# First loads over two queues, an early weight load and late third query tiles at the start of an attention and gMLP kernel

## The chip, the cores and the metric

The kernel runs on one core of one Trainium2 chip. The metric is the device time of one execution in microseconds (us); lower is better. Profiles are of single executions, with times counted from the first instruction of the span. Below, PE is the engine of matmuls and transposes, DVE, ACT and POOL are the vector, scalar and GpSimd engines, SP is the engine that mostly issues transfers. POOL and ACT can issue transfers too; all transfers run on the same 16 DMA engines.

## What is computed

Grouped-query attention (8 batches, 16 query heads over 4 key and value heads, 384 positions, head dimension 64), then a gated MLP with a spatial gate over its output:

```python
scores = scale * np.matmul(q, k.transpose(0, 1, 3, 2))      # k, v repeated 4 times over heads
attn = softmax(scores)
x = np.matmul(attn, v) -> (batch, 384, 1024)
h = np.maximum(x @ w_in, 0.0)                                # w_in 1024 x 1024
u, v = h[..., :512], h[..., 512:]
v_n = (v - mean(v)) / np.sqrt(var(v) + 1e-06)
v_s = np.einsum('ts,bsd->btd', w_spatial, v_n) + b_spatial[None, :, None]
out = ((u * v_s) @ w_out)                                    # w_out 512 x 1024
```

Inputs and output are fp32; the matmuls work on fp16 copies.

## The kernel before

The scheduling is manual: each engine executes its instructions in the order in which the Python program emits them, and waits on semaphores where an operand, a buffer or an issued transfer isn't ready.

A batch has 6 sets: 3 query tiles `t` of 128 positions, times 2 pairs `j` of key heads. A set has 3 units, one for each key tile. A unit (`units`, L254) is two score matmuls (L268, one for each key head of the pair), followed by two exponentials on ACT (`exp`, L280). After the three units of a set, `weigh` (L282) multiplies the exponentials by the values (L288, two groups `hh` of 12 matmuls), and DVE takes a reciprocal (L301) and multiplies by it (L303): that gives a part of `x`. `x_turn` (L314) transposes `x` on PE and DVE copies it out of PSUM (L207). Then the MLP: `v_part` (L336, the second 512 columns of `w_in`, matmul L343), `u_part` (L397, the first 512 columns, L402), the spatial matmul (L421) and the output matmul (L453).

The MLP's matmuls are filler: the generator `gated` (L472) yields them one at a time and `pour` (L639) puts them between attention units so far as a budget in ns allows. The first 21 units run one at a time (loop at L660, `ALONE`). In that loop, work listed in `todo` for step `u` is emitted after the step's scores and exponentials. For the first batch, the first half of `v_part`'s contraction (4 of 8 steps) may be poured from step 7, the second half from step 10 (L478, L480).

The start, which the change touches:

- L136 to L143 load the first batch: a key load in two halves, the value load, and query loads by `part_q` (L117), one transfer for some heads `hs` and tiles `ts` of pair `j`. One query load is issued by ACT, all others by SP. The last two (L142, L143) hold tiles 1 and 2 of a pair, 512 KB each.
- `cast_k` (L173), `cast_q` (L187) and `cast_v` (L180) copy fp32 loads to fp16; the engine is an argument. L554 to L557 cast the first key half and the first query tile on DVE and the second key half on POOL.
- `k_turn` (L209) and `q_turn` (L223) transpose keys and queries on PE (L215, L229) and copy the result out of PSUM. `idle` (L546) emits matmuls whose result nobody reads.
- L564 to L587 are POOL's queue: it issues the load of `w_in` (`load_w_in`, L152; columns by half, rows by range of 128; fp32 to fp16 in the transfer) in four pieces, the loads of the second batch, and casts. `load_w_in(1, 0, 4)` holds what the first four `v_part` matmuls read, `load_w_in(1, 4, 8)` what the next four read.
- L588 to L611 list what each step of the first 21 gets in addition: casts on DVE, `q_turn` of each tile, `x_turn`.

Of the kernel before, what the change touches and what calls it, by code (L numbers as in the profile page):

```python
# [17 lines left out]
def kernel(  # L18
# [21 lines left out]
    NT = S // P  # L40
# [29 lines left out]
    pool, dve, act, sp = nc.gpsimd, nc.vector, nc.scalar, nc.sync  # L70
# [27 lines left out]
    stage = {}  # L98

    def stage_tile(n, b, j=None):  # L100
        shape = [P, 2, NT, G * D] if n == "q" else [P, HKV, NT * D]
        t = ld.tile(
            shape, FP32, name=f"{n}32_{b}_{j}", tag=f"{n}32", bufs=4 if n == "q" else 2
        )
        stage[n, b, j] = t
        return t

    def part(src, t, lo, hi, eng):
        eng.dma_start(t[:, lo:hi, :], src[lo:hi].rearrange("h (p t) d -> p h (t d)", t=NT))

    def load_k(b, eng=sp):
        part(k[b], stage_tile("k", b), 0, HKV, eng)

    def load_v(b, eng=sp):
        part(v[b], stage_tile("v", b), 0, HKV, eng)

    def part_q(b, j, hs, ts, eng):  # L117
        h0, h1, t0, t1 = hs[0], hs[-1] + 1, ts[0], ts[-1] + 1
        eng.dma_start(  # L119
            stage["q", b, j][:, h0:h1, t0:t1],  # L120
            q[b, 8 * j + 4 * h0 : 8 * j + 4 * h1].rearrange(
                "(h i) (c t r) d -> (i c) h t (r d)", i=G, t=NT, r=G
            )[:, :, t0:t1],
        )

    def load_q(b, j, eng=sp):
        stage_tile("q", b, j)
        part_q(b, j, (0, 1), (0, 1, 2), eng)
# [8 lines left out]
    part(k[0], k0, 0, 2, sp)  # L137
    part_q(0, 0, (0,), (0,), sp)
    part(k[0], k0, 2, 4, sp)
    part_q(0, 1, (0, 1), (0,), sp)  # L140
    part(v[0], v0, 0, HKV, sp)
    part_q(0, 0, (0, 1), (1, 2), sp)  # L142
    part_q(0, 1, (0, 1), (1, 2), sp)  # L143

    w_in16 = cst.tile([P, NK, DFF], FP16, name="w_in16")
    w_out16 = cst.tile([P, NM, DM], FP16, name="w_out16")
# [5 lines left out]
    def load_w_in(half, lo, hi):  # L152
        cols = slice(half * DH, (half + 1) * DH)
        pool.dma_start(
            w_in16[:, lo:hi, cols],
            moe_w_in[lo * P : hi * P, cols].rearrange("(t p) f -> p t f", p=P),
        )
# [12 lines left out]

    k16s, q16s, kTs, qTs = {}, {}, {}, {}

    def cast_k(b, eng, js=(0, 1)):  # L173
        if b not in k16s:
            k16s[b] = ld.tile([P, 2, NT, 2, D], FP16, name=f"k16_{b}", tag="k16")
        src = stage["k", b, None].rearrange("p (j h) (t d) -> p j t h d", h=2, t=NT)
        for j in js:
            eng.tensor_copy(k16s[b][:, j], src[:, j])

    def cast_v(b, eng, js=(0, 1)):  # L180
        g0, g1 = 2 * js[0], 2 * js[-1] + 2
        eng.tensor_copy(
            v1[b % 2][:, g0:g1, :, 0:D].rearrange("p g t d -> p (g t) d"),
            stage["v", b, None][:, g0:g1].rearrange("p g (t d) -> p (g t) d", t=NT),
        )

    def cast_q(b, j, eng, ts=None, hs=(0, 1)):  # L187
        if (b, j) not in q16s:
            q16s[b, j] = ld.tile([P, NT, G, 2, D], FP16, name=f"q16_{b}_{j}", tag="q16", bufs=4)
        t16 = q16s[b, j]  # L190
        src = stage["q", b, j].rearrange("p h t (r d) -> p h t r d", d=D)
        for hh in hs:
            if ts is None:
                eng.tensor_copy(t16[:, :, :, hh, :], src[:, hh])  # L194
            else:
                for t in ts:
                    eng.tensor_copy(t16[:, t, :, hh, :], src[:, hh, t])
# [313 lines left out]
    b32 = cst.tile([P, S], FP32, name="b32")  # L511
    ws32 = cst.tile([P, NT, S], FP32, name="ws32")
    ws16 = cst.tile([P, NT, NT, P], FP16, name="ws16")

    def load_spatial(eng):
        eng.dma_start(b32, moe_b_spatial.rearrange("(a s) -> a s", a=1).to_broadcast([P, S]))
        rows = moe_w_spatial.rearrange("(c t r) s -> r c t s", t=NT, r=G)
        for r in range(G):
            eng.dma_start(ws32[32 * r : 32 * r + 32], rows[r])

    def cast_spatial():
        pool.tensor_copy(
            bias_bc.rearrange("a (t r c) -> a t r c", t=NT, r=G),
            b32.rearrange("a (c t r) -> a t r c", t=NT, r=G),
        )
        for tt in range(NT):
            pool.tensor_copy(
                ws16[:, :, tt].rearrange("p s (r c) -> p s r c", r=G),
                ws32[:, tt].rearrange("p (c s r) -> p s r c", s=NT, r=G),
            )  # L530

    def send_spatial():
        sp.dma_start_transpose(
            wsT16.rearrange("p s (t c) -> p (s t) c", t=NT),
            ws16.rearrange("p s t c -> p (s t c)"),
        )
# [4 lines left out]
    def at(n, f, *args):  # L541
        todo.setdefault(n, []).append((f, args))

    idle_no = [0]

    def idle(count):  # L546
# [4 lines left out]
        for _ in range(count):  # L551
            nc.tensor.matmul(ps, ident16, ident16, start=True, stop=True)

    cast_k(0, dve, (0,))  # L554
    cast_q(0, 0, dve, (0,), (0,))
    cast_q(0, 0, dve, (0,), (1,))
    cast_k(0, pool, (1,))  # L557
    idle(28)
    k_turn(0, 0, act)
# [1 line left out]
    q_turn(0, 0, 0, dve)  # L561
    idle(8)

    load_w_in(1, 0, 4)  # L564
    cast_v(0, pool)
    load_w_in(1, 4, 8)
    cast_q(0, 1, pool, (1,))
    load_k(1, pool)
    load_q(1, 0, pool)
    cast_q(0, 1, pool, (2,))  # L570
    load_q(1, 1, pool)
    load_v(1, pool)
    load_w_in(0, 0, 4)
    load_w_in(0, 4, 8)
    pool.memset(b32[:, 0:1], 0.0)
    pool.memset(ws32[:, 0, 0:1], 0.0)
    load_spatial(sp)
    cast_k(1, pool)
    load_k(2, pool)
    cast_q(1, 0, pool)  # L580
    load_q(2, 0, pool)
    cast_q(1, 1, pool)
    load_q(2, 1, pool)
    cast_v(1, pool)
    load_v(2, pool)
    cast_spatial()
    send_spatial()  # L587
    at(2, cast_q, 0, 1, dve, (0,))  # L588
    at(2, k_turn, 0, 1, dve)
    at(2, idle, 16)  # L590
    for n, b, j, t in (
        (2, 0, 1, 0),
        (5, 0, 0, 1),
        (6, 0, 0, 2),
        (7, 0, 1, 1),
        (9, 0, 1, 2),
        (16, 1, 0, 0),
        (18, 1, 1, 0),
        (20, 1, 0, 1),
        (21, 1, 1, 1),  # L600
        (24, 1, 0, 2),
        (27, 1, 1, 2),
    ):
        at(n, q_turn, b, j, t, dve)
    at(2, idle, 8)
    at(3, cast_q, 0, 0, dve, (1,))
    at(4, cast_q, 0, 0, dve, (2,))
    at(15, k_turn, 1, 0, dve)
    at(18, k_turn, 1, 1, dve)
    for s in range(SETS):  # L610
# [128 lines left out]
```

## Time and profile before

| | us |
|---|---|
| median of 3 runs | 242.28 |
| lowest and highest | 241.59, 246.64 |
| the profiled execution | 242.07 |
| its span, first to last instruction | 240.2 |
| PE busy | 232.8 (97%) |
| ACT busy | 170.4 (71%) |
| DVE busy | 142.0 (59%) |
| POOL busy | 100.4 (42%) |

The granted clock of PE is 1.000 over the span. In the profile a line such as `6.34 0.50 POOL L178 CAST k<-k_None ...` gives the start, the duration, the engine, the line of the kernel, the operation and its operands; in brackets stands how long the engine was idle before it, and what released it. The chain of waits follows the work that ended last back to its start, each step to what released it. The time from issue to landing of a transfer is given in a list of its own.

### The profile page before, as it was taken

To read this page: it belongs to the slowest core of one execution; us is meant where nothing else is said; L and a number is where in the kernel's file an instruction comes from. 1 tells how busy PE (TensorE), PEld (TensorE's weight loads), DVE (VectorE), ACT (ScalarE), POOL (GpSimd) and SP (SyncE) were. 2 spreads that over 40 slices of the span, in tenths; PEclk is the share of its full clock that TensorE was granted. 3 is DMA by queue.
4 is the path that set the end of the run, shared out by engine and by line. 5 is a ranking of instruction groups with operands and counts; after the bars stand their busy time and mean duration, and the time that the engine had idled before them with its cause. 6 is when DMAs were issued, how large, how long until landed. Compare 5 with 4: busy or idle time off the path is not lost.

```text
span 240.2 us, 5910 instructions
## 1 busy us (share of the span) xinstructions
PE 232.8 (97%) x2322; PEld 124.9 (52%) x2322; DVE 142.0 (59%) x375; ACT 170.4 (71%) x348; POOL 100.4 (42%) x138
## 2 busy tenths in 40 slices
PE   7889999999999999999999999999999999999993
PEld 6554656554555455554455445555455445545541
DVE  1567767566536765475844767366744767467361
ACT  2889997888798678978797776987587776501211
POOL 1598758531554900367025810556013500370550
PEclk9999999999999999999999999999999999999999
DMA  5999999999999959996999499939922434240157
GB/s 145 312 269 320 262 360 135 178 232 274 318 146 317 275 154 183 290 244 167 174 256 264 140 220 263 312 115 155 237 42 44 112 120 122 44 175 4 59 202 263
DMA packets 65339, 47.47 MB, mean 198 GB/s; under 512 B 48160, under 2 KB 57440, under 8 KB 65312
## 3 DMA queue, kind: packets, MB, share of 16 engines
q1 hardware_dynamic: 61488, 39.10, 66.5%
q0 software_dynamic: 3680, 7.87, 13.5%
q8 instruction: 18, 0.29, 0.5%
q10 hardware_dynamic: 144, 0.13, 0.3%
q14 instruction: 9, 0.07, 0.1%
HBM read 25.95 MB, written 12.58 MB: 160 GB/s over the span
## 4 chain that ended last, share of the span: by engine, by line
PE 91%; DMA 5%; DVE 1%; SPq 0%; ACT 0%; issue 0%; POOL 0%
PE pu L402 18%; PE pv L343 18%; PE po L453 18%; PE sc L268 15%; PE av L288 14%; PE psp L421 7%; DMA w_in<-in_moe_w_in_dram 3%; DMA k_None<-in_k_dram 2%; PE qps L229 1%; DVE x L303 1%; PE xps L320 0%; DVE vr L357 0%; ACT osb L207 0%; DVE r L301 0%; SPq L119 0%
## 5 line engine op out<-in xcount | busy, mean ns | idle before, releaser
L280 ACT ACTIVATE aT<-sc 128x512 f16<-128x512 f32 x288 | 148.2, 610 | 32.9 <-PE sc L268 31.8
L288 PEld LDWEIGHTS <-aT 128*128 128x128 f16 x1152 | 47.7, 97 | 18.1 <-issue 2.3
L288 PE MATMUL av<-v,aT 128*128 128x65 f16 x1152 | 51.7, 193 | 0.7 <-DVE x L303 0.6
L343 PE MATMUL pv<-w_in,xt 128*128 128x512 f16 x192 | 50.8, 379 | 0.5 <-DMA w_in<-in_moe_w_in_dram 0.5
L453 PE MATMUL po<-w_out,gT 128*128 128x512 f16 x192 | 50.4, 379 | 0.0
L402 PE MATMUL pu<-xt,w_in 128*128 128x384 f16 x256 | 49.9, 326 | 0.0
L387 POOL TENSOR_SCALAR vn<-vr,rstd,nmr 128x512 f16<-128x512 f32 x23 | 17.7, 784 | 73.2 <-DVE nmr L382 39.6
L438 POOL TENSOR_TENSOR gT<-vs,uT 128x384 f16<-128x384 f32 x31 | 32.5, 1059 | 33.9 <-DVE r L301 17.1
L268 PE MATMUL sc<-qT,kT 64*128 64x512 f16 x288 | 42.3, 380 | 0.4 <-DVE qT L207 0.2
L303 DVE TENSOR_TENSOR x<-av,r 128x256 f16<-128x256 f32 x96 | 40.8, 425 | 3.3
L301 DVE RECIPROCAL r<-av 128x4 f32<-128x4 f32 x96 | 17.2, 179 | 43.0 <-PE av L288 42.8
L207 DVE COPY osb<-po 128x512 f32<-128x512 f32 x38 | 26.1, 686 | 17.2 <-PE po L453 17.2
L402 PEld LDWEIGHTS <-w_in 128*128 128x128 f16 x256 | 22.1, 97 | 17.1 <-issue 5.5
L413 ACT ACTIVATE uT<-pu 128x384 f16<-128x384 f32 x32 | 15.8, 494 | 16.3 <-PE pu L402 16.1
L453 PEld LDWEIGHTS <-gT 128*128 128x128 f16 x192 | 17.1, 97 | 17.5 <-issue 3.3
L343 PEld LDWEIGHTS <-xt 128*128 128x128 f16 x192 | 15.8, 97 | 18.4 <-issue 5.6
L194 POOL CAST q<-q 128x768 f16<-128x768 f32 x28 | 22.4, 832 | 6.5 <-DMA q<-in_q_dram 6.5
L268 PEld LDWEIGHTS <-kT 64*128 64x128 f16 x288 | 10.8, 94 | 25.1 <-issue 14.4
L421 PE MATMUL psp<-wsT,vn 128*128 128x384 f16 x96 | 22.2, 327 | 0.0
L433 DVE TENSOR_TENSOR vs<-psp,bias_bc 128x384 f32<-128x384 f32 x32 | 17.6, 552 | 7.1 <-PE psp L421 6.9
L357 DVE TENSOR_SCALAR vr<-pv 128x512 f32<-128x512 f32 x24 | 16.4, 683 | 8.4 <-PE pv L343 8.4
L369 DVE BATCH_NORM_STATS2 stats<-vr 128x6 f32<-128x512 f32 x24 | 16.4, 685 | 0.1
(44 smaller groups left out, 94.7 us busy)
## 6 DMA issues: line engine op xcount, KB each, us to landing
out_dram<-osb SPq DMA_DIRECT2D x21, 512.0 KB, 2.9
q<-in_q_dram SPq DMA_DIRECT2D x10, 768.0 KB, 7.4
q<-in_q_dram POOLq DMA_DIRECT2D x4, 768.0 KB, 10.5
v_None<-in_v_dram SPq DMA_DIRECT2D x6, 384.0 KB, 4.6
w_in<-in_moe_w_in_dram POOLq DMA_DIRECT2D x4, 512.0 KB, 11.0
k_None<-in_k_dram SPq DMA_DIRECT2D x5, 384.0 KB, 3.9
out_dram<-osb SPq DMA_DIRECT2D x6, 256.0 KB, 2.2
q<-in_q_dram SPq DMA_DIRECT2D x2, 512.0 KB, 7.7
```

The costliest lines, as they stand in the source:

```text
L194: eng.tensor_copy(t16[:, :, :, hh, :], src[:, hh])
L207: (act.copy if eng is act else dve.tensor_copy)(o, i)
L268: nc.tensor.matmul(sc, kTs[b][rows, j, kt * P : (kt + 1) * P], qTs[b, j][rows, qt].rearrange("p (r i c) -> p i r c", r=G, i=G), start=True ...
L280: act.activation(a, sc, AF.Exp, scale=scale)
L288: nc.tensor.matmul(av[:, i * (D + 1) : (i + 1) * (D + 1)], aT[:, kt, hh, i * P : (i + 1) * P], v1[b % 2][:, 2 * j + hh, kt, 0 : D + 1], st ...
L303: dve.tensor_tensor(x16s[b][:, qt, c : c + 256].rearrange("p (i d) -> p i d", i=G), o[:, :, 0:D], r.to_broadcast([P, G, D]), ALU.mult,)
L343: nc.tensor.matmul(pv, xts[b][:, kt, st * P : (st + 1) * P], w_in16[:, kt, DH:DFF], start=(kt == 0), stop=(kt == NK - 1),)
L387: (dve if b == 0 and st == 1 else pool).tensor_scalar(vn, v_r.pop((b, st)), rstd[:, st : st + 1], nmr[:, st : st + 1], op0=ALU.mult, op1=A ...
L402: nc.tensor.matmul(pu[:, 0:S], w_in16[:, kt, m * P : (m + 1) * P], xts[b][:, kt, :], start=(kt == 0), stop=(kt == NK - 1),)
L421: nc.tensor.matmul(psp[:, 0:S], v_n[b, st][:, m * P : (m + 1) * P], wsT16[:, st, :], start=(st == 0), stop=(st == NT - 1),)
L438: pool.tensor_tensor(gT, vs, uT, ALU.mult)
L453: nc.tensor.matmul(po, gTs[b][:, m, tt * P : (tt + 1) * P], w_out16[:, m, half * 512 : (half + 1) * 512], start=(m == 0), stop=(m == NM - 1),)
```

## The change

Five edits at the start of the program:

1. The first tile of query pair 1 is issued by ACT, behind ACT's first load, and no longer by SP.
2. SP's last two query loads hold tile 1 alone (256 KB each). Tile 2 of both pairs is loaded by `rest_q`, emitted at step 2: DVE writes one element of the target in each partition (a memset), and SP's transfer, which overwrites it, waits for that memset.
3. The cast of the first key half is split over its two heads: POOL casts the second head, DVE the first.
4. `load_w_in(1, 0, 4)` stands on POOL right behind its part of that cast, ahead of POOL's cast of the second key half.
5. In the list of steps the third tiles are later: `q_turn` of pair 0's tile 2 at step 10 (was 6) and of pair 1's at step 12 (was 9), pair 1's tile 1 at step 6 (was 7), and DVE's cast of pair 0's tile 2 at step 7 (was 4). The rest of POOL's queue from `cast_q(0, 1, pool, (2,))` on is emitted at step 3 and not before the loop; its order stays.

```diff
     part(k[0], k0, 2, 4, sp)
-    part_q(0, 1, (0, 1), (0,), sp)
+    part_q(0, 1, (0, 1), (0,), act)
     part(v[0], v0, 0, HKV, sp)
-    part_q(0, 0, (0, 1), (1, 2), sp)
-    part_q(0, 1, (0, 1), (1, 2), sp)
+    part_q(0, 0, (0, 1), (1,), sp)
+    part_q(0, 1, (0, 1), (1,), sp)
...
-    def cast_k(b, eng, js=(0, 1)):
+    def cast_k(b, eng, js=(0, 1), hs=slice(0, 2)):
...
-            eng.tensor_copy(k16s[b][:, j], src[:, j])
+            eng.tensor_copy(k16s[b][:, j, :, hs], src[:, j, :, hs])
...
+    def rest_q(j):
+
+        dve.memset(stage["q", 0, j][:, 0:1, NT - 1, 0:1], 0.0)
+        part_q(0, j, (0, 1), (NT - 1,), sp)
...
-    cast_k(0, dve, (0,))
+    cast_k(0, pool, (0,), slice(1, 2))
+    load_w_in(1, 0, 4)
+    cast_k(0, dve, (0,), slice(0, 1))
     cast_q(0, 0, dve, (0,), (0,))
     cast_q(0, 0, dve, (0,), (1,))
     cast_k(0, pool, (1,))
...
-    load_w_in(1, 0, 4)
     cast_v(0, pool)
     load_w_in(1, 4, 8)
     cast_q(0, 1, pool, (1,))
     load_k(1, pool)
     load_q(1, 0, pool)
-    cast_q(0, 1, pool, (2,))
-    load_q(1, 1, pool)
...
+    def behind_rest():
+        cast_q(0, 1, pool, (2,))
+        load_q(1, 1, pool)
...
+    at(3, behind_rest)
...
         (2, 0, 1, 0),
         (5, 0, 0, 1),
-        (6, 0, 0, 2),
-        (7, 0, 1, 1),
-        (9, 0, 1, 2),
+        (10, 0, 0, 2),
+        (6, 0, 1, 1),
+        (12, 0, 1, 2),
...
+    at(2, rest_q, 0)
+    at(2, rest_q, 1)
     at(3, cast_q, 0, 0, dve, (1,))
-    at(4, cast_q, 0, 0, dve, (2,))
+    at(7, cast_q, 0, 0, dve, (2,))
```

More of the change, by code (lines that the diff above doesn't have):

```diff
@@ L569 @@
     load_q(1, 0, pool)
-    cast_q(0, 1, pool, (2,))
-    load_q(1, 1, pool)
[L572 to L587, printed above, removed]
+    def behind_rest():
+        cast_q(0, 1, pool, (2,))
+        load_q(1, 1, pool)
+        load_v(1, pool)
+        load_w_in(0, 0, 4)
+        load_w_in(0, 4, 8)
+        pool.memset(b32[:, 0:1], 0.0)
+        pool.memset(ws32[:, 0, 0:1], 0.0)
+        load_spatial(sp)
+        cast_k(1, pool)
+        load_k(2, pool)
+        cast_q(1, 0, pool)
+        load_q(2, 0, pool)
+        cast_q(1, 1, pool)
+        load_q(2, 1, pool)
+        cast_v(1, pool)
+        load_v(2, pool)
+        cast_spatial()
+        send_spatial()
+    at(3, behind_rest)
     at(2, cast_q, 0, 1, dve, (0,))
```

## The prediction

> **What bounds the kernel now.** I read the page first, then busy time by stretch, then the chain of waits over the first 34 us, then the start on DVE and POOL and the single DMA issues there. All in us. The profiled execution took 242.07 with a span of 240.2; its sum is the base here. The median of the three runs shown is 242.28, 0.21 above it.
>
> Busy time by stretch (start:end, length, then busy time and count per engine, granted clock, DMA share, GB/s):
>
> ```profile
> 6.46:15.27 8.81, 7.29 (x99) 4.67 (x100) 5.42 (x18) 8.18 (x16) 6.15 (x11) 1.00 1.13 268
> 15.27:36.00 20.73, 20.67 (x265) 11.12 (x266) 14.14 (x44) 18.78 (x37) 14.98 (x24) 1.00 1.12 319
> 36.00:235.00 199.00, 198.75 (x1910) 104.56 (x1908) 120.34 (x309) 140.78 (x293) 78.33 (x97) 1.00 0.77 182
> ```
>
> From 15.27 to 235 PE idles 0.3 in all, at a granted clock of 1.00. So PE is the bound after 15.27, and the end moves by what PE starts earlier there, less what work is pushed behind that point. Ahead of it much of PE's busy time is filler (`idle`). The chain says what ended the start:
>
> ```profile
> 1.76 4.52 DMA k_None<-in_k_dram
> 6.28 0.05 issue
> 6.34 0.45 POOL k L178
> 6.78 8.35 DMA w_in<-in_moe_w_in_dram
> 15.13 0.14 issue
> 15.27 0.38 PE pv L343
> ```
>
> The first half of w_in's second 512 columns is issued by POOL behind the cast of the second key half, lands at 15.13 and releases the first `pv` matmul. PE's own wait there is only 0.5; the other paths arrive shortly before. These are on DVE and POOL:
>
> ```profile
> 10.53 0.90 DVE L197 CAST q<-q 128x256 f16<-128x256 f32 x4 [1.18 <-DMA q<-in_q_dram]
> 11.56 0.42 DVE L303 TENSOR_TENSOR x<-av,r 128x256 f16<-128x256 f32 x1
> 11.90 0.41 DVE L207 COPY qT<-qps 128x512 f16<-128x512 f16 x1
> ...
> 6.34 0.50 POOL L178 CAST k<-k_None 128x384 f16<-128x384 f32 x1 [4.91 <-DMA k_None<-in_k_dram]
> 6.78 0.96 POOL L154 DMA_DIRECT2D w_in<-in_moe_w_in_dram  x1
> ...
> 9.98 0.75 POOL L154 DMA_DIRECT2D w_in<-in_moe_w_in_dram  x1
> 11.92 0.75 POOL L197 CAST q<-q 128x256 f16<-128x256 f32 x2 [1.19 <-DMA q<-in_q_dram]
> ```
>
> DVE waited 1.18 and POOL 1.19 for the query loads, so those are nearly as late as w_in. The DMA issues (each asked for alone; last number: issue to landing) give the landings: q pair 0 at 3.26 + 7.2, pair 1 at 3.81 + 8.1 = 11.9, w_in's loads at 15.1 and 17.7, b at 17.84 + 8.0.
>
> ```profile
> q<-in_q_dram SPq DMA_DIRECT2D x1, 256.0 KB, 4.9
> q<-in_q_dram SPq DMA_DIRECT2D x1, 512.0 KB, 7.2
> q<-in_q_dram SPq DMA_DIRECT2D x1, 512.0 KB, 8.1
> w_in<-in_moe_w_in_dram POOLq DMA_DIRECT2D x1, 512.0 KB, 8.4
> w_in<-in_moe_w_in_dram POOLq DMA_DIRECT2D x1, 512.0 KB, 7.7
> b<-in_moe_b_spatial_dram SPq DMA_DIRECT2D x1, 192.0 KB, 8.0
> ```
>
> DMA share is 1.13 in 6.46 to 15.27: the DMA engines are full, so an earlier load pushes another back. What they moved, over 0 to 30 in 40 slices of 0.75:
>
> ```profile
> GB/s 0 0 22 234 359 243 82 220 341 350 374 395 369 258 212 197 190 169 180 200 326 354 347 380 363 377 389 391 307 292 214 229 262 279 252 257 231 216 255 332
> ```
>
> Query loads run at up to 395, w_in alone (from 10.5) at 170 to 210.
>
> **The change, part by part.**
>
> *Key cast split, w_in behind half of it.* The first key half lands at 4.03. DVE's cast of it (0.55) halves, POOL does the other half in about 0.25 (half of 0.50). w_in is issued at about 4.03 + 0.25 = 4.3 instead of 6.78. With its own latencies (7.7 to 8.35) it lands at 12.0 to 12.6; with all of the SP queue's remaining loads ahead, 14 at most, by my estimate. The first `pv` no longer waits for it unless everything else is over 1.3 earlier. POOL's second key cast now stands behind a 0.96 issue, which ends at 5.3, before its data at 6.28: free.
>
> *SP's order, ACT's second issue.* Third query tiles (512 KB of 1024 KB) leave the first queue; pair 1's first tile goes to ACT, behind an issue of 0.42, ahead of ACT's first copy at 5.17: ACT is free. SP's later issues come 0.5 earlier. The tile on ACT competes with the first key half and the first query tile. Bounds for the first exp (6.87 now): 0.1 earlier (shorter key cast, then the query casts) to 0.4 later (256 KB at the 359 GB/s peak of the DMA row, 0.7, half of it ahead). Neither is paid on: `av` of the first pair starts at 10.09 behind the value cast (ends 10.04), and the fifth exp it needs ends at 9.4, 0.6 before. 0.
>
> *Less on DVE before the first x.* Only the second tiles are cast at 10.53: two casts (0.49, as the pair at 4.50) for four (0.90). The reciprocal, `x` and `qT` copy behind them come 0.41 earlier if the query loads land as now.
>
> *The first pv.* PE ends the `av` ahead of it at 14.73 (14.20 + 0.53). Four transposes of a third tile (0.33 a group in the chain) move behind it: 14.40. DVE's 0.41: 13.99. The query loads are the unknown. Best, they are not slowed and each is half as large: 0.7 earlier (512 KB took 1.4, the distance of the two landings, and half of it goes). Worst, all 512 KB of w_in go ahead of the last of them: at the 190 GB/s of 11 to 14 in the DMA row that is 2.75, less the 1.4 of third tiles that no longer stand ahead, 1.4 later. I take 0.35 later, the middle: 14.34. So 15.27 - 14.34 = 0.93 earlier, of which 0.33 is work given back: **0.60 gained**.
>
> *The second w_in load.* It is issued as now, 9.98, because the value cast stands ahead of it. The same bytes as before have to pass ahead of it, so I leave it at 17.68. The fifth `pv` matmul, its first reader, starts at 18.62 now; with 0.60 gained and the other third-tile group (0.33) behind it, it is wanted at 17.69. It becomes the next limit, so the gain can't be much over 0.6: I charge 0.1. Bounds: 0 (0.7 sooner) and 0.6 (0.6 later, the whole gain).
>
> *Third tiles behind a memset on DVE.* Two memsets (0.06 each, as the one at 0.81) stand after the `qT` copy that ends at 9.35; SP issues at about 9.6 and 10.1 (0.5 each). In front of `r` and `x` of the second pair DVE now casts pair 0's third tile (0.49), in order. If it lands by 14.5, DVE is through in time. 256 KB took 4.9: 14.5. I charge 0.05; the upper bound is under the rivals. POOL's cast of the other third tile now waits too; behind it stand seven things (loads of batch 1's second queries and values, w_in's other half twice, two memsets, then SP's b and w_spatial). I estimate them 1 to 2 later. Readers with slack: w_in's other half landed by 32.4 for the first `pu` at 36, w_spatial's transpose landed at 40.1 for 44.7. 0, but only while POOL's queue still has a backlog of transfers, which it had until 32.
>
> **Sum:** 242.07 - 0.60 + 0.10 + 0.05 = **241.6**.
>
> **A rule against the change.** POOL's first w_in issue took 0.96 while DVE cast two query tiles beside it, one of which took 0.50 where the other casts took 0.29; the second issue, with DVE idle, took 0.75. In the new order the issue at 4.3 stands again beside DVE's two casts at 4.5, so 0.2 on each, within the cover of 0.6 above. The Trainium skill, "SBUF — State Buffer", section on SBUF's two separate sides, says that a DVE fp32 copy within SBUF can lock GpSimd out of a shared port for the whole instruction, so that descriptors can't be written. By that rule the issue could lose both casts, 0.57 instead of 0.2, and w_in would land by 13.2; the sum would not change, since the first `pv` is at 14.34.
>
> **Rivals.**
>
> *R1, slower: the third tile blocks DVE.* b, sent by SP while POOL's transfers filled the DMA engines, took 8.0 for 192 KB. If the third tile does too, it lands at 17.6; cast, reciprocal and `x` (0.49 + 0.18 + 0.42 and gaps, 1.15) end at 18.8. The scores that take over that bank start at 16.82 now and would be unmoved at 16.71 (one `pv` more, 0.22, one transpose group less, 0.33, ahead). With the second `x` behind, 2.3 lost: **244.4**. It decides from a latency of about 5.8 on (landing 15.4). For it: that row. Against: in b's case POOL had seven transfers in flight, here one or two.
>
> *R2, no change: w_in takes its room from the second query tiles.* Pair 1's land 1.4 later, at 13.3; POOL casts until 14.0, then transposes, turn of x, scores, `av` (0.33 + 0.33 + 0.32 + 0.48): first `pv` at 15.5, 0.2 later, plus 0.33 given back: **242.6**. For it: DMA share 1.13. Against: the two 512 KB query loads landed 1.4 apart, their full rate, although w_in had been issued 3.7 before the first of them landed. The Trainium skill, "DMA: Bandwidth & Descriptors", "Queues, rings and completion order", states that a DMA engine takes turns between the queues that have work; by that rule this rival is what would happen.
>
> *R3, more: both query loads come 0.7 earlier*, and the second w_in load 1.0, as the DMA engines lose less in the dip to 82 GB/s at 4.5: first `pv` at 13.3, so 1.97 less 0.33 gained, less the 0.1: **240.5**.
>
> *The change does nothing to w_in:* excluded, since nothing but the key half at 4.03 stands ahead of the issue.
>
> **From this to the numbers.** A measurement of this kernel tells about 2% (4.8) from no change. Forecast 241.6: chance 0.50. R2 242.6: 0.20. R1 244.4: 0.17, with its effect growing from 0 at a latency of 5.8. R3 240.5: 0.13. The range 240.4 to 243.4 holds the forecast, R2, R3 and R1 up to a latency of 7. Faster by over 2% would be under 237.4: 0.01. Slower by over 2%, over 247.1, would need a third tile 11 late: 0.03. Within: 0.96.
>
> **What would show it.** w_in's issue at 4.3 and landing at 12 to 14; first `pv` at 14.0 to 14.6, released by something other than w_in; two query casts on DVE at about 10.5; DVE's wait for the third tile under 0.5 and its landing by 14.5; PE without idle after 17.8. The prediction is wrong if DVE sits over 1 on that cast, if POOL's cast of pair 1 ends after 13.5, or if PE stalls later than 36, which nothing here foresees.

## The result, and the profile after

The changed kernel is slower: a median of 249.59 us (247.51 to 251.26, 6 runs) against 242.28 (241.59 to 246.64, 6 runs), a ratio of 1.0286 with a 95% interval of 1.0215 to 1.0357. I had forecast 241.6. The profiled execution took 251.26 (span 249.1), 9.2 over the 242.07 of the profiled execution of before; it is the highest of the six, so some 1.7 of that is this execution's own.

The ratios here leave out executions that are over 1.5% above the fastest of their kernel (the profiled one of the changed kernel is one, by a hair), which matters for E2, E3, E11 and E13, where the spread is given.

Busy time by stretch of the changed kernel; the columns are those of the same view of before, and the third stretch is new:

```profile
6.46:15.27 8.81, 8.46 (x115) 5.24 (x113) 4.93 (x16) 7.82 (x17) 4.26 (x7) 1.00 1.14 233
15.27:36.00 20.73, 17.61 (x241) 9.86 (x239) 14.14 (x44) 16.65 (x33) 13.33 (x22) 1.00 0.87 231
36.00:64.00 28.00, 23.30 (x229) 12.05 (x227) 14.07 (x40) 17.38 (x37) 14.07 (x19) 0.94 1.16 199
64.00:244.00 180.00, 179.75 (x1704) 93.90 (x1703) 107.72 (x274) 125.39 (x261) 66.79 (x82) 1.00 0.73 180
```

PE, which idled 0.06 from 15.27 to 36, now idles 3.1 there and another 4.7 between 36 and 64; behind 64 nothing is lost. DMA share in the second stretch fell from 1.12 to 0.87: the DMA engines themselves ran dry for a while. PE's own lines that carry a wait of 0.9 or more, with the first `pv` ahead of them:

```profile
14.13 0.59 PE L343 MATMUL pv<-w_in,xt 128*128 128x512 f16 x2
...
18.12 0.39 PE L268 MATMUL sc<-qT,kT 64*128 64x512 f16 x2 [2.16 <-DVE x L303]
...
27.11 0.40 PE L229 MATMUL qps<-ident,q 128*128 128x128 f16 x4 [0.96 <-POOL q L194]
```

```profile
55.00 0.38 PE L453 MATMUL po<-w_out,gT 128*128 128x512 f16 x1 [1.75 <-DMA w_out<-in_moe_w_out_dram]
...
58.27 1.46 PE L268 MATMUL sc<-qT,kT 64*128 64x512 f16 x6 [2.89 <-DMA qT<-q]
```

Four waits, 7.8 in all. The chain of waits names what stands behind them:

```profile
9.98 7.01 DMA q<-in_q_dram
17.02 0.50 DVE q L197 x2
17.64 0.44 DVE x L303
18.12 0.39 PE sc L268 x2
...
20.09 0.75 POOL q L197 x2
20.84 0.66 POOL q L119
...
26.21 0.86 POOL q L194
27.11 0.40 PE qps L229 x4
...
44.28 13.95 DMA qT<-q
58.27 1.46 PE sc L268 x6
```

The casts of the third tiles on DVE and POOL, and POOL's next load:

```profile
17.02 0.50 DVE L197 CAST q<-q 128x256 f16<-128x256 f32 x2 [3.06 <-DMA q<-in_q_dram]
...
20.09 0.75 POOL L197 CAST q<-q 128x256 f16<-128x256 f32 x2 [8.44 <-DVE qT L207]
20.78 0.72 POOL L119 DMA_DIRECT2D q<-in_q_dram  x1
```

The same load, and the transposes of batch 2's queries, in the kernel before:

```profile
14.74 0.72 POOL L119 DMA_DIRECT2D q<-in_q_dram  x1
...
39.98 9.79 SPq L246 DMA_TRANSPOSE qT<-q  x2
```

SP sends for pair 0's third tile at 9.98 and it lands 7.01 later; DVE, in order, sits on its cast for 3.06, and `x` and the scores come late. Pair 1's third tile lands at 19.97, after 9.5; POOL, in order, waits for it from 11.6 to 20.09. (The profile names a DVE copy that ended in the same moment; in E10 and E11 below the same cast starts 0.13 after its tile lands, too.) So POOL's next load (batch 1's second query pair) goes out at 20.78, where the kernel before issued it at 14.74: 6.0 later. All of POOL's queue is late from there, up to its casts for batch 2, which SP's transposes of batch 2's queries follow: the first is issued at 44.28, before at 39.98. It landed at 50.5 before, for scores that started at 50.67: 0.2 of slack. Now it lands at 58.2. Of these 7.8, 4.3 are the later issue; the other 3.5 are a longer transfer (13.95 for 10.49), and why is open.

The start of the n-th of the 288 exponentials on ACT, against the kernel before (a count in the two traces; positive is later), shows where the loss comes in:

| exponential | before | after | difference |
|---|---|---|---|
| 12 | 12.94 | 13.29 | +0.36 |
| 18 | 17.31 | 18.61 | +1.30 |
| 30 | 23.92 | 25.36 | +1.44 |
| 36 | 27.27 | 29.74 | +2.47 |
| 66 | 47.06 | 49.80 | +2.73 |
| 72 | 51.16 | 58.95 | +7.80 |
| 78 | 55.36 | 64.38 | +9.02 |
| 287 | 204.79 | 213.90 | +9.11 |

2.5 are lost by exponential 36 (start 27.27 before), on DVE's wait and on POOL's late casts for batch 1; 6.3 are lost between 49.8 and 64.4. The waits of PE there sum to 4.6. The rest is the clock:

```profile
58.00:60.00 2.00, 1.73 (x7) 0.43 (x7) 0.00 (x0) 1.05 (x3) 0.00 (x0) 0.50 1.25 271
60.00:62.00 2.00, 2.00 (x18) 1.14 (x17) 0.80 (x3) 2.00 (x5) 0.00 (x0) 0.67 0.93 271
```

The granted clock (the number behind the engines' busy times) is one half right after the idle time. By the clock records it is exactly 0.5 for 3.41 us, from 57.90 on, so 1.7 more. The Trainium skill, "TensorE: Matmul & The Clock Gate", section "What's actually happening", says that the clock halves after at least one idle window of about 3.4 us. The length agrees with these records, but here a window that was idle in part was enough. In each trace the clock changes on a grid of 3.41 us. In the window of that grid ahead of a fall to one half, PE idled 3.04 here, and 1.90 (E10), 2.42 (E12), 2.55 (E9), 2.73 (E5), 3.04 (E4) and 3.41 (E3) in the experiments below; after windows at full clock in which it idled 1.73 or less, the clock stayed. The wait of 2.16 ahead of 18.12 fell on two windows, 0.98 and 1.18, and halved nothing.

### The profile page after: what moved, and what is told of

It reads as the page before. It is cut to its first block, busy times and chain, and to the rows that moved or that the text cites. A ratio compares the mean times of both kernels' runs of the same rounds, so it can differ in the third digit from the quotient of the medians.

```text
span 249.1 us, 5917 instructions
## 1 busy us (share of the span) xinstructions
PE 235.2 (94%) x2322; PEld 125.7 (50%) x2322; DVE 142.6 (57%) x377; ACT 170.0 (68%) x348; POOL 100.5 (40%) x139
## 4 chain that ended last, share of the span: by engine, by line
PE 82%; DMA 10%; POOL 3%; DVE 2%; issue 1%; ACT 0%; SPq 0%; POOLq 0%
PE po L453 17%; PE pu L402 16%; PE pv L343 15%; PE sc L268 13%; PE av L288 12%; PE psp L421 6%; DMA qT<-q 6%; DMA q<-in_q_dram 4%; PE qps L229 1%; DVE x L303 1%; PE idle L557 1%; POOL w_in L154 0%; DVE qT L207 0%; POOL q L194 0%; DVE q L197 0%
## 5 line engine op out<-in xcount | busy, mean ns | idle before, releaser
L453 PE MATMUL po<-w_out,gT 128*128 128x512 f16 x192 | 51.1, 383 | 1.8 <-DMA w_out<-in_moe_w_out_dram 1.8
L268 PE MATMUL sc<-qT,kT 64*128 64x512 f16 x288 | 43.3, 385 | 5.4 <-DMA qT<-q 2.9
```

What stands on the lines that cost most here:

```text
L268: nc.tensor.matmul(sc, kTs[b][rows, j, kt * P : (kt + 1) * P], qTs[b, j][rows, qt].rearrange("p (r i c) -> p i r c", r=G, i=G), start=True ...
L453: nc.tensor.matmul(po, gTs[b][:, m, tt * P : (tt + 1) * P], w_out16[:, m, half * 512 : (half + 1) * 512], start=(m == 0), stop=(m == NM - 1),)
```

## The experiments

The theory after this reading (A): nothing is wrong with the early weight load; the loss is the two in-order queues that wait for a late third tile, DVE's and above all POOL's. The rival (B): the loads at the front, w_in or the tile on ACT, take room from others. Where an expectation below gives the letter B to another rival, it says which. "After" below is the changed kernel. The kernel before took 241.27, 241.33, 241.95 and 241.04 (medians) beside the four groups of runs.

### One part at a time: E1 to E4

E1, after without the memset:

```diff
     part_q(0, 1, (0, 1), (1,), sp)
+    part_q(0, 0, (0, 1), (2,), sp)
+    part_q(0, 1, (0, 1), (2,), sp)
...
-    at(2, rest_q, 0)
-    at(2, rest_q, 1)
```

> The changed kernel, but the third query tiles are sent for right behind the second ones, without the memset; all else as changed, POOL's order and the later steps too. Theory A (two queues blocked by the late third tiles: DVE's cast costs PE 2.2 us near 16 us, and POOL's cast holds up its loads until 20 us, which costs 5.7 us later): neither wait, what is left is the earlier first pv matmul, so 241.3 us (240.5 to 242.5), POOL's cast done before 16 us. Theory B (w_in's early load and ACT's second load take room from all other loads, and that costs the time): still 245 us or more.

E2, after with POOL's cast further back:

```diff
-        cast_q(0, 1, pool, (2,))
         load_q(1, 1, pool)
...
         load_spatial(sp)
+        cast_q(0, 1, pool, (2,))
         cast_k(1, pool)
```

> The changed kernel, but POOL's cast of pair 1's third tile stands behind its issues of batch 1's loads and w_in's other half, and ahead of its cast of batch 1's keys. Theory A: the stalls of PE near 27 and 54 to 60 us go, the one near 16 us stays: 243.6 us (242.8 to 244.5). Theory B: nothing was waiting on POOL that matters, 248 to 250 us.

E3, before with edits 2 and 5 alone (late third tiles behind the memset, their casts and transposes at the steps of after):

> The kernel before with the late third tiles alone (memset, later steps); w_in's first load, the key cast and ACT's loads are as before. Theory A: both blocked queues are there and the early w_in's gain isn't: 249 us or more (248 to 252). Theory B: 242 to 243.5 us.

E4, before with edits 3 and 4 alone (split cast, early w_in load):

> The kernel before with the split key cast and w_in's first load behind POOL's part of it, nothing else. Theory A: no queue is blocked; w_in lands by 13 us, the query loads up to 1.4 us later: 241.3 to 242.9 us. Theory B: 245 us or more.

Measured:

| | median (range) | ratio (95%) |
|---|---|---|
| E1 | 241.75 (240.49 to 242.76) | 1.0031 (1.0000 to 1.0062) |
| E2 | 247.08 (242.07 to 250.79) | 1.0078 (1.0044 to 1.0112) |
| E3 | 251.23 (247.50 to 254.09) | 1.0296 (1.0233 to 1.0359) |
| E4 | 242.56 (241.05 to 248.83) | 1.0033 (1.0001 to 1.0064) |

The late tiles alone make the whole loss (E3; its ratio rests on 247.50 and 248.91, the other two executions took 253.56 and 254.09); without them the rest costs about 0.3% (at most 0.6% by the intervals) and gains nothing (E1, E4). B falls. E2's ratio rests on three of its eight runs, 242.07 to 243.56; the other five took 245.7 to 250.8, so moving POOL's cast helped in some executions only, where A had 242.8 to 244.5. The mean granted clock of those five is 0.986 or 0.993: one half for 3.41 of some 245 us makes 0.993, so PE stalled there too, once or twice. In the profiled one (242.07) the tiles landed early, 5.4 after the issue for the first.

How the loss is shared between the two queues differs between executions. In E3's profiled one (248.91) the first tile landed after 10.0, DVE sat 6.10 on its cast, and PE waited

```profile
21.02 0.61 PE L268 MATMUL sc<-qT,kT 64*128 64x512 f16 x2 [5.19 <-DVE x L303]
```

and lost 5.5 by exponential 30; it lost 1.2 behind that, though POOL's load went out at 21.28 (6.5 later than before) and the first query transpose at 44.70 (4.7 later).

### Both casts moved, or the memset moved: E5, E6

E5 is E2 with DVE's cast moved too:

```diff
-    at(7, cast_q, 0, 0, dve, (2,))
+    at(9, cast_q, 0, 0, dve, (2,))
```

> The changed kernel with both casts that wait for a late third tile moved back: POOL's behind its five issues and two memsets, and DVE's from step 7 to step 9. The transfers and the memset stay as they are. Theory A (the loss is what stands in line behind the two waiting casts): DVE's second x of the first batch comes before the tile's landing, so PE's stall of 2.2 near 17 goes, POOL's issues go out near 14 to 16, batch 2's query transposes are issued by 40.5; 241.5 to 243, as long as the third tiles land by 17 or so; if they land at 20, the transposes of the tile stall PE by up to 1 instead. Theory B (the loss lies in DMA contention of the late transfers themselves, whoever waits): still over 246. Beside the run that moved POOL's cast alone (1.0078 of the time before), A gives 0.5 to 1.5 less than that run.

E6, after with the memsets and the two sends at step 0:

```diff
-    at(2, rest_q, 0)
-    at(2, rest_q, 1)
+    at(0, rest_q, 0)
+    at(0, rest_q, 1)
```

> The changed kernel with the two memsets at step 0 instead of step 2, so that they run near 6.7 and SP issues the third tiles near 6.8 and 7.4, ahead of POOL's second w_in load (8.75) and not 1.2 behind it. Casts and steps stay. Theory A, with its part on queues (a transfer of SP starts only when what POOL has issued before it has drained): only the first w_in load and the second query tiles are in flight ahead, the third tiles land at 12 to 14, DVE's and POOL's casts wait under 1, PE does not stall before 36; 241.3 to 242.5. Rival C (the dependency itself is dear: SP's transfer behind a memset of DVE takes 7 or more from issue to landing wherever it stands): landings at 14 to 17, a stall of PE over 1, 244 or more.

E5 took 249.06 (248.46 to 249.66), 1.0318 (1.0287 to 1.0349): no better than after, so theory A failed as I had put it. It fits the rival of that expectation, contention of the late transfers themselves. E6 took 242.90 (240.93 to 244.33), 1.0046 (1.0016 to 1.0075), 0.4 above A's range and below rival C's 244; its third tiles landed at 12.71 and 13.47, inside A's 12 to 14, so the dependency on the memset is not dear by itself.

E5's casts, on DVE and on POOL:

```profile
21.90 0.50 DVE L197 CAST q<-q 128x256 f16<-128x256 f32 x2 [4.38 <-DMA q<-in_q_dram]
...
24.97 0.74 POOL L197 CAST q<-q 128x256 f16<-128x256 f32 x2 [11.16 <-DMA q<-in_q_dram]
```

POOL's loads now went out by 13.6, as meant, but the tiles, sent for at 11.30 and 11.77, landed 10.6 and 13 later. The waiting cast in after had kept POOL's later loads off the DMA engines; with it out of the way they are issued ahead of the tiles or just behind them, and move beside them. From 17 to 20 in E5 the two queues (q0 is POOL's, q1 SP's; packets, MB, share of the DMA engines) stand so:

```profile
q0 software_dynamic: 191, 0.98, 84.2%
q1 hardware_dynamic: 192, 0.19, 19.3%
```

One packet for one packet, but POOL's are mostly 4608 and 6144 bytes here and the tile's 1024: the tile gets a sixth of the bytes. This is the turn-taking by packet that the Trainium skill describes ("DMA: Bandwidth & Descriptors", "Queues, rings and completion order"), and the counts agree. (A packet of these records is one contiguous run; the page's packet holds several descriptors, which these records don't show.) In after, between 10 and 13.4, there is no turn-taking, though SP had issued at 9.98; the only queue is

```profile
q0 software_dynamic: 533, 0.53, 113.8%
```

and the tiles' first packet starts at 13.52, when the last 1024-byte packets of w_in's second load, issued 1.2 ahead of the tiles, run out. SP's transfer got no turn for 3.5 us; whether its work already lay in the queue by then, the trace doesn't show. In E1, where SP issues the third tiles at 4.04 and 5.21, beside the first w_in load (4.37) and far ahead of the second, they got their turns (9 to 12: 447 packets on q0, 265 on q1). It looks the same the other way round: in after, w_in's first load, issued at 4.27, got its first packet at 7.31, 3.0 later, when 169 of the 2048 packets (768 and 1024 bytes) of SP's and ACT's earlier loads were left; POOL's load at 20.78, with the DMA engines nearly idle, got its first after 1.4.

### Where E1's head start went: E7, E8

In its profile E1 was 1.16 ahead of the profiled kernel before at 45 and 0.70 ahead behind batch 2's query transposes. E7 is E1, and E8 the kernel before, with these transposes sent for earlier:

```diff
+        early = 1 if b == 2 else 0
-        at(u0 - 12, k_send, b)
-        at(u0 - 10, q_send, b, 0)
+        at(u0 - 12 - early, k_send, b)
+        at(u0 - 10 - 3 * early, q_send, b, 0)
...
-        at(u0 - 8, q_send, b, 1)
+        at(u0 - 8 - 2 * early, q_send, b, 1)
```

> The changed kernel with the third tiles sent right behind the second ones (no memset), and with batch 2's transposes sent for earlier: key and first query transpose emitted at step 23 (24 and 26 before), the second query transpose at step 26 (28), so that on SP they stand ahead of the first transpose of x that is issued at 35.3. Theory A (the start does gain some 1.1, which is lost again where PE waits at 50 for batch 2's query transposes): the first query transpose goes out 2 to 3 earlier, scores at 50 don't wait, and the gain stays: 240.5 to 241.2, ratio about 0.995 to 0.998. If the gain is lost elsewhere or was none: 241.5 to 242, the same as without this edit. If earlier transposes slow the loads that are still in flight: slower than 242.

> The kernel before with the same earlier sends of batch 2's transposes and nothing else. In its profile the scores at 50.67 start as the transposes land, without a wait of PE, so in undisturbed runs nothing is to be gained: 241 to 241.6, ratio 0.998 to 1.001. It is the control for the run above: theory A gives that run 0.5 to 1.1 less than this one. If this one gains as much, the gain comes from the sends and not from the early start.

E7: 242.59 (241.21 to 245.38), 1.0049 (1.0024 to 1.0073). E8: 243.31 (241.23 to 245.32), 1.0071 (1.0047 to 1.0095). Both are slower than the kernel before, the control too, and their intervals overlap: no hidden gain appears. The earlier sends cost something, and why is not shown. That there is no head start to find is seen in E8's start, which is that of before, unchanged:

```profile
14.19 0.38 PE L343 MATMUL pv<-w_in,xt 128*128 128x512 f16 x1 [0.47 <-DMA w_in<-in_moe_w_in_dram]
```

The first `pv` is at 14.19 there, and at 13.65 and 13.88 in E12 and E13, whose start is unchanged as well, and where it doesn't wait for w_in. With the early w_in load it is at 14.13 (after), 13.86 (E1) and 14.09 (E4): not earlier. In the profiled kernel before it was at 15.27. Of that, 0.54 was the wait for w_in, whose last of 16 parts landed at 15.13 and the one before it at 14.23. The rest was late already: the query loads landed at 11.87, for 10.61 to 10.81 in E8, E12 and E13, and the `av` ahead of the first `pv` started at 14.20, for 13.20 to 13.51. The head start was against one late start in one execution.

### The tiles' place among the transfers: E9 to E11

E9 has no memset; POOL itself issues the third tiles:

```diff
     cast_q(0, 1, pool, (1,))
+    part_q(0, 0, (0, 1), (2,), pool)
+    part_q(0, 1, (0, 1), (2,), pool)
     load_k(1, pool)
```

> The changed kernel without the memset, and with the third tiles issued by POOL, between its casts of pair 1's second tile and its load of batch 1's keys: at about 10 and 11, as late as SP issues them in the changed kernel, but in POOL's own queue, where nothing that POOL issues later can pass or share. Casts and steps stay. The run that moved both casts back (its third tiles landed 10.6 after their issue, while POOL's packets of 4608 and 6144 bytes moved beside their packets of 1024 bytes) has changed theory A: what costs is the tiles' place among the transfers, first behind POOL's w_in load and then packet by packet against packets six times as large. By this theory A2 the tiles land here 15 to 16.5, DVE's wait is 1 to 2, PE's under 1, POOL's cast ends by 17; 241.8 to 243.5, and the runs don't scatter. If any third tile issued near 10 is late (theory A as it stood: no room, whatever the queue): landings at 17 to 20, 246 or more.

E10 moves `load_k(1, pool)` and `load_q(1, 0, pool)` behind POOL's cast of the third tile:

> The changed kernel with POOL's loads of batch 1's keys and of its first query pair (packets of 4608 and 6144 bytes) behind its cast of the third tile, so that none of them moves beside the third tiles. Memset, casts and steps stay. Theory A2: the tiles still start only as the second w_in load drains, near 13.5, then have the DMA engines alone: 512 KB in 1.3 to 1.6, landed by 15.0 to 15.5 both, 1.5 to 4.5 earlier than in the changed kernel, and POOL's cast ends by 16.2; PE's stall near 17 is under 1. Batch 1's loads come 4 to 6 later instead, so that PE stalls near 27 and at 50 to 60 and the total is no forecast of mine: 243 to 250; the landings are the test. If the tiles land at 17 or later with nothing beside them, the sharing by packets is not the cause.

E11 exchanges two lines:

```diff
-    load_w_in(1, 4, 8)
     cast_q(0, 1, pool, (1,))
+    load_w_in(1, 4, 8)
```

> The changed kernel with POOL's second w_in load behind its cast of pair 1's second tile instead of ahead of it: issued at about 10.2, just after SP's first third tile (10.0) and not 1.2 ahead of it. Theory A2, first half (a transfer on SP's queue that was empty starts only when what POOL has issued has drained): at 10.0 only the end of the first w_in load is ahead, the tiles' first packets come at 11 to 12 and not at 13.5, and both land by 14.5 to 16; DVE waits under 1.5, PE under 1. The second w_in load lands at 17 to 18 (15.4 in the changed kernel), a wait of up to 0.7 on PE; 242 to 244. If the tiles start at 13.5 again or later: the delay is the transfer's own, whatever is ahead of it, and the total stays over 247.

| | median (range) | ratio (95%) | first packet on SP's queue after the issue | casts of third tiles start, DVE and POOL |
|---|---|---|---|---|
| after | 249.59 | 1.0286 (1.0215 to 1.0357) | 3.5 | 17.02, 20.09 |
| E9 | 245.63 (244.81 to 248.04) | 1.0158 (1.0088 to 1.0228) | | 15.56, 16.34 |
| E10 | 245.86 (245.20 to 248.42) | 1.0171 (1.0102 to 1.0240) | 3.4 | 15.96, 16.77 |
| E11 | 246.54 (243.14 to 249.12) | none: two near 243.7, two near 249.0 | 1.0 | 14.53, 18.41 |

The landings came out about as theory A2 had them. Without large packets beside them (E10) both tiles come close together, at 15.93 and 16.64, the second 3.3 earlier than in after, though 0.4 and 1.1 later than the 15.5 I had written, and PE's stall near 17 was 1.9 and not under 1. With w_in's second load issued only 0.3 ahead (E11) their first packet starts 1.0 after the issue and not 3.5; the first tile lands at 14.51, but the second still meets the large packets and lands at 18.28, where I had 16 at most. On POOL's own queue (E9) they land within the range I gave. The times of E9 and E11 missed, by 2 and more. E9 shows why. POOL was 2.3 later than before behind its cast (its load at 17.02 for 14.74), the transposes of batch 2 were issued 1.2 later, at 41.16, and took 1.9 longer (12.40), and PE, until then even with the kernel before (0.02 ahead at exponential 66), lost 4.4, a wait and then a half clock:

```profile
53.60 1.47 PE L268 MATMUL sc<-qT,kT 64*128 64x512 f16 x6 [2.88 <-DMA qT<-q]
```

### POOL late, with no tile late: E12, E13

This holds POOL up in the kernel before, by work that nobody reads (E12 with six casts, E13 with two):

```diff
     cast_q(0, 1, pool, (2,))
+    pad32 = cst.tile([P, 768], FP32, name="pad32")
+    pad16 = cst.tile([P, 768], FP16, name="pad16")
+    pool.memset(pad32, 0.0)
+    for _ in range(6):
+        pool.tensor_copy(pad16, pad32)
     load_q(1, 1, pool)
```

> The kernel before with POOL held up by work that nobody reads: a memset and six casts of 128x768 (0.83 each by the casts of that shape) on a tile of their own, between its cast of pair 1's third tile and its load of batch 1's second query pair. Loads, memsets and waits of the start are as before; only the seven things behind, and all of POOL's later queue, are some 5 later, as far as POOL has no slack there (in the changed kernel the same load was 6.0 later). Theory A3 (POOL's delay by itself, whatever caused it, is the larger part of the loss, since batch 2's query transposes follow POOL's casts and have no slack at 50): transposes issued 3 to 4.5 later than 39.98, PE waits 2 to 3.5 for them and for w_out between 50 and 60, a lower granted clock there, and a wait near 27 for POOL's cast of batch 1's queries; 246 to 248.5. If the stall of DVE near 17, or the late tiles' traffic, is what carries the loss: under 243.5.

> The same with a memset and two casts of 128x768, 2.5 in all, which is what POOL was late by in the run with the third tiles on POOL's queue (2.3 later than in the kernel before, 1.0158 of its time). Theory A3: transposes issued 1 to 1.5 later, PE waits 1 to 3 for them; 243 to 246. If POOL's queue has that much slack, as my prediction assumed: 241.5 to 242.5, the time before.

E12: 245.80 (244.94 to 246.66), 1.0188 (1.0148 to 1.0229), 4.8 above the kernel before, 0.2 short of the range of A3 and well above the other theory's 243.5. E13: 243.92 (240.94 to 246.09), 1.0115 (1.0081 to 1.0149). Its ten runs scatter (the ratio rests on six, up to 244.22; the other four took 244.94 to 246.09), and the profiled one (240.94) shows no wait, so a delay of 2.5 costs in some executions and not in others.

In E12 POOL's load went out at 19.70, 5.0 later than in the profiled kernel before, and nothing was lost up to exponential 30, so the added casts themselves cost PE nothing there. The loss is mostly not where I had put it. The transposes were issued at 42.83, 2.9 later, but PE was by then itself 2.7 later and waited only 0.2 for them. The loss is on batch 1's queries:

```profile
26.03 0.61 PE L229 MATMUL qps<-ident,q 128*128 128x128 f16 x4 [1.84 <-POOL q L194]
```

With 1.0 for POOL's key cast just ahead of it, and the half clock that follows

```profile
26.00:28.00 2.00, 1.97 (x19) 1.27 (x19) 1.03 (x3) 0.00 (x0) 2.00 (x3) 0.50 1.05 205
28.00:30.00 2.00, 2.00 (x22) 1.12 (x21) 0.61 (x2) 1.16 (x3) 2.00 (x4) 0.75 1.10 245
```

4.3 are lost between exponentials 30 and 36. So POOL's queue, late by 5.0 where the late tile made it 6.0, is worth 4.8 by itself, against 7.3 for the whole change. It doesn't simply add to DVE's part: in after, DVE's wait had already made PE later at 27, so less was lost there and more at 58; in E5, where DVE waited 4.38, PE was 6.2 later by exponential 30 and lost nothing behind it. A piece of work stalls PE only by as much as it is later than PE already is.

## Why the prediction was wrong, point by point

- **w_in's issue, landing and the first pv: right in place, empty in value.** Issued at 4.27 (4.3 forecast), landed at 11.8 (12.0 to 12.6), first `pv` at 14.13 (14.34), not released by w_in. But the term "0.60 gained" was taken against 15.27, a late start of one execution; with the start unchanged the first `pv` came at 13.65 to 14.19 in three other executions. E1 and E4 gain nothing.
- **The second w_in load, R2 and R3:** it landed at 15.4 and held nothing up. The second query tiles landed at 8.66 and 9.36 and were not pushed back, so R2 did not happen. They and the second w_in load came 1.9 to 2.5 earlier than before, more than R3 had, and yet the first `pv` was at 14.13 and not at 13.3, so R3's gain did not follow. What held it there was not settled.
- **"Neither is paid on" (the tile on ACT):** the first exponential came 0.58 later (7.45 for 6.87), outside the bound of 0.4: SP's first query tile landed at 5.08 for 4.37 beside ACT's. E1, which keeps it, is 0.3% over before, so it is no large term.
- **"256 KB took 4.9: 14.5. I charge 0.05": failed.** The first third tile took 7.0, and 5.4, 10.0 and 10.6 in E2, E3 and E5. I priced it by its bytes, from a row in which nothing stood ahead of it. It waited 3.5 for its first packet, behind w_in's second load, and then shared packet by packet with larger packets. R1 had the mechanism, at a chance of 0.17, from b's 8.0, and I set that row aside because "here one or two" transfers were ahead. Those were enough: by E10 and E11 it is what POOL had issued ahead, and the size of its packets, that counts, and not the number of transfers. But at 7.0 R1's own sum gives 243.4, the edge of the range; what lay beyond it is the next two steps.
- **"I estimate them 1 to 2 later ... 0": failed, and this took the time out of the range.** POOL's queue came 6.0 later, and the price was not 0. I had checked two readers with slack, w_in's other half (36) and w_spatial's transpose (44.7), and left out the casts of batch 1's queries (27) and the transposes of batch 2's (landed 50.5 for 50.67, issued behind POOL's casts). My condition, that POOL's queue still had a backlog, failed too: from 18 to 20.7 the DMA engines were nearly idle (a share of 0.14). E12 measures 4.8 for the queue by itself.
- **The clock:** I priced waits by their length. Here and in E3, E5, E9, E10 and E12 a long wait brought a granted clock of one half for 3.41, up to 1.7 more. No row of before could show it, since PE did not idle so long there before its work ended.
- **The rule on the shared port:** no test, and the reading of its row was wrong. w_in's issue took 0.94 again, but DVE was casting during 0.14 of it only, since the query tile landed late. In the 15 traces this first w_in issue takes 0.94 to 0.99, with DVE's casts beside it for 0.04 (E5, 0.945) or for 0.74 (E8, 0.945); the second takes 0.75 to 0.81. So the 0.2 belongs to the first issue and not to the casts; why is open, and a lock that lasts a whole cast is not seen.
- **The list of what would make it wrong** was the right list: DVE sat 3.06 on the cast, POOL's cast of pair 1 ended at 20.8, and PE stalled behind 36, which, I wrote, nothing there foresaw. The row of batch 2's transposes did.

## What to carry to other kernels

When a load is moved behind another engine's signal, price its latency by what is queued ahead of it and beside it at that moment, in packets, and then go down the whole queue of each engine that waits for it, in order, to the last reader with no slack; waits of PE that filled 1.9 or more of one clock window of 3.41 us cost a halved clock on top. Before a gain is built on one late landing in one profile, look at whether it is late in other executions.

## What the runs showed that I had not expected

- SP's 256 KB third tile got its first packet 1.0 (E11), 1.9 (E2), 3.0 (E6), 3.4 (E10), 3.5 (after), 3.6 (E3) and 4.3 us (E5) after its issue, each time when most of a w_in load issued well ahead of it had gone: 350 (E10) to 508 (E5) of its 512 packets of 1024 bytes, all 512 in E2. A w_in load issued behind it (E6), or only 0.3 to 0.5 ahead (E11, E2), did not hold it up. Why the two queues take no turns until then is open; that the order of issue decides is what these runs fit, and no run here was made for it alone but E11.
- Taking away a wait made its cause worse: with POOL's cast moved (E5) the tiles landed 10.6 and 13 after the issue, for 7.0 and 9.5.
- Batch 2's first query transpose landed 10.4 after its issue in E2 (39.74) and 14.3 in E4 (40.58). In E4's profiled execution (248.83), with POOL and SP nearly on time, PE waited 2.5 for them and 2.4 for w_out, and had two windows of half clock, 6.83 in all. What makes them slow was not settled. The kernel before itself took from 240.4 to 248.9 in its 24 executions beside E1 to E4, its longest with a mean clock of 0.986 or 0.993, so it has such stalls too; no trace of one is kept.
- No version here beats the kernel before; E1, without the late tiles, comes nearest (1.0031).
